# Four bf16 sums of the vector engine placed ahead of one fp32 add, in five slots of a fused attention and MLP kernel

## The chip, the cores and the metric

The kernel runs on one core of one Trainium2 chip. The metric is the device time of one execution in microseconds (us); the figure of a kernel is the median of its runs. The engines are called as in the profile: PE (matrix multiply), PEld (its weight loads), DVE (vector), ACT (scalar, activation functions), POOL (GpSimd) and SP (here only a DMA queue). L723 is line 723 of the kernel's file.

## What is computed

Inputs are `x` (8 batches, 8 heads, 512 tokens, 64 wide), `state` (8, 8, 32, 64), `w_in` (512 x 2048) and `w_out` (2048 x 512). Per batch and head:

```
a     = softmax(x @ state^T / 8);   xread = a  @ state      # 512 rows
a2    = softmax(state @ x^T / 8);   sread = a2 @ x          # 32 rows
rows  = concat(xread, sread), heads side by side            # 544 x 512 per batch
out   = gelu(rows @ w_in) @ w_out                           # exact gelu
```

The output is 4352 x 512 in fp32. Nearly all the work is the two products with `w_in` and `w_out`.

## The kernel before

**Staging.** The program is written out by hand in the order in which every engine is to run it: each engine takes its own instructions in program order, and semaphores join the engines. After a start phase (batches 0 and 1) the loop at L1224 runs over batches b = 2 to 7, and in each over eight slots p = 0 to 7. A slot holds two hidden tiles of batch b and one product that finishes batch b-1.

**Hidden tiles, `M(k)` (`mm1`, L501).** Two PE matmuls of 128x512 into a PSUM tile `hp`, then a Gelu on ACT into `gs[b][:, m, :]` (L513). Sixteen tiles m make a batch. The left operand is `P`, which is `state @ w_in` of the batch. `hp` shares a ring of four PSUM buffers (`ps_f`, tag `f`) with other tiles, half of the `P` products among them.

**Second matmul, `X(b, name)` (L672).** The 512 x 2048 by 2048 x 512 product of a batch is cut in a Strassen-Winograd scheme into seven products named "1" to "7", each of sixteen 128x256 matmuls (L647) into one of four PSUM banks (`otile` 0 to 3). Their left operands are quarters of `g` or sums of quarters (`g_sum`, L629). Products "1", "6", "5", "7" of batch b-1 run in slots 0 to 3 of batch b, product "3" in slot 5, and product "4" of batch b itself in slot 7. After product "7" DVE makes two adds (`c22`, `c21`, L702 and L705). After product "3" it makes one add, `oh <- xp, u` (L699, recorded at L666), which reads PSUM bank 2 and is followed by an output DMA on SP.

**Product "2"** of batch b is done by a second level of the same scheme (`sub_a`, L738, and `sub_b`, L745; matmuls of 128x128 at L729). It needs four sums of bf16 pieces of 128x512 elements, named 5, 6, 7, 3 in that order (`sub_sums`, L715; the DVE instruction is L723, tile `gsub`). They read only tiles m = 0 to 7 of batch b, which are done by slot 3. Sum 6 reads sum 5, sum 3 reads sum 6. `sub_a` uses sum 5, `sub_b` the other three.

**Slots 3 to 6 in batches 2 to 6, in program order:** slot 3: `M` tiles, product "7" with its two adds, then sum 5 (L1264). Slot 4: two tiles. Slot 5: two tiles with product "3" (in odd batches between the two tiles) and its add (L1296); then sums 6, 7, 3 (L1299); then `p_all` (L988), which makes `P` of the next batch: in even batches first the `reads_mm` products (L964), then four groups f of eight matmuls (L441) into PSUM tiles, where group 3's first tile is bank 2, then six copies to bf16 (L1004), three on ACT and three on DVE; then `rearr_ones` (L235), two bf16 copies on POOL, which wait in even batches for the `reads_mm` products that read their target and in odd ones for a `hold` on a Gelu; then `sub_a`; then two more ACT copies (L1310). Slot 6: two tiles, `sub_b`. The second hidden tile of slot 6 takes the PSUM buffer that the first DVE copy of `p_all` empties.

POOL also does `rearr` (L225), two bf16 copies, once an `x` batch has landed.

Of the kernel before, what the change touches and what calls it, by code (L numbers as in the profile page):

```python
# [10 lines left out]
BF16 = mybir.dt.bfloat16  # L11
# [6 lines left out]
def kernel(  # L18
# [8 lines left out]
    nc = tc.nc  # L27
# [17 lines left out]
    apool = ctx.enter_context(tc.tile_pool(name="apool", bufs=3))  # L45
# [230 lines left out]
    def xtr_dma(b):  # L276
        A = atts[b]
        nc.sync.dma_start_transpose(
            out=A.xT.rearrange("p j c n -> p (j c) n"),
            in_=A.x4.rearrange("p j c n -> p (j c n)"),  # L280
        )
# [43 lines left out]
    def scores(b, half):  # L325
        A = atts[b]
        if half == 0:
            begin_e(b)
        pt = ps_f.tile([128, SJ, 2, 2, NS], FP32, name="pt", tag="f")
        for ci in range(2):  # L330
            c = 2 * half + ci
            for j in range(SJ):
                nc.tensor.matmul(  # L333
                    pt[:, j, :, ci, :],
                    lhsT=A.xT[:, j, c, :],
                    rhs=sbd[:, b, c, :],
                    start=True,
                    stop=True,
                )
        nc.scalar.activation(  # L340
            out=A.e[:, :, 64 * half:64 * half + 64],
            in_=pt.rearrange("p j t c n -> p (j t) (c n)"),
            func=AF.Exp,
            scale=scale,
        )

    def norm(b, half):
        A = atts[b]
        G = SJ * 2
        hs = slice(64 * half, 64 * half + 64)  # L350
        e4 = A.e[:, :, hs].rearrange("p g (c n) -> p g c n", n=NS)
        cs = att.tile([128, G, 2], FP32, name="cs", tag="cs")
        nc.vector.reduce_sum(out=cs, in_=e4, axis=AX.X)  # L353
        ics = att.tile([128, G, 2], FP32, name="ics", tag="ics")
        nc.vector.reciprocal(out=ics, in_=cs)
        nc.vector.tensor_tensor(  # L356
            out=A.a[:, :, hs].rearrange("p g (c n) -> p g c n", n=NS),
            in0=e4,
            in1=ics[:, :, :].to_broadcast((128, G, 2, NS)),
            op=ALU.mult,  # L360
        )
# [16 lines left out]
    def atr_dma(b):  # L378
        A = atts[b]
        A.AT = att.tile([128, SJ, 2, 128], BF16, name="AT", tag="AT")  # L380
        nc.sync.dma_start_transpose(
            out=A.AT.rearrange("p j t n -> p (j t) n"), in_=A.a
        )
# [173 lines left out]
    MH = MC // 2  # L557
# [44 lines left out]
    xs = {}  # L602
# [12 lines left out]
    def chain(name, q, got):  # L615
        a11, a12, a21, a22 = q(0, 1), q(0, 0), q(1, 1), q(1, 0)
        return {
            "1": (a11,),
            "2": (a12,),
            "4": (a22,),  # L620
            "5": (a21, a22, ALU.add),
            "6": (got.get("5"), a11, ALU.subtract),
            "7": (a11, a21, ALU.subtract),
            "3": (a12, got.get("6"), ALU.subtract),
        }[name]
# [3 lines left out]
    def g_sum(b, names, home=None):  # L629
        got = g_lhs.setdefault(b, {})  # L630
        for name in names:
            x, y, op = chain(name, lambda h, k: g_q(b, h, k), got)
            if home is None:
                got[name] = apool.tile([128, MH, 256], BF16, name="gsum", tag="gsum")
            else:
                got[name] = home
            nc.vector.tensor_tensor(out=got[name], in0=x, in1=y, op=op)  # L637
# [70 lines left out]
    def sub_q(b):  # L708
        def q(h, k):
            g = g_q(b, 0, 0)  # L710
            return g[:, MH // 2 * k:MH // 2 * k + MH // 2, 128 * h:128 * h + 128]

        return q

    def sub_sums(b, names):  # L715
        if "5" in names:
            xs[b, "subs"] = apool.tile([128, 4, MH // 2, 128], BF16, name="gsub", tag="gsum")
            xs[b, "sub"] = {}
        got = xs[b, "sub"]
        for name in names:  # L720
            x, y, op = chain(name, sub_q(b), got)
            got[name] = xs[b, "subs"][:, "5673".index(name)]
            nc.vector.tensor_tensor(out=got[name], in0=x, in1=y, op=op)  # L723

    def sub_mm(b, name, at, start=False):
        lhs = chain(name, sub_q(b), {})[0] if name in "124" else xs[b, "sub"][name]
# [174 lines left out]
    def r_homes():  # L901
        pair = [att.tile([128, 2, MH, 128], BF16, name="rs", tag="xT") for _ in range(2)]
        homes = [pair[0][:, 0], pair[0][:, 1], pair[1][:, 0], pair[1][:, 1]]
        rs["homes"] = dict(zip("5673", homes))
        rs["lhs"] = {}

    def r_sum(names):
        got = rs["lhs"]
        for name in names:
            x, y, op = chain(name, r_q, got)  # L910
            got[name] = rs["homes"][name]
            nc.vector.tensor_tensor(out=got[name], in0=x, in1=y, op=op)
# [104 lines left out]
    def hold_for(b, m):  # L1017
        nc.gpsimd.tensor_copy(out=hold, in_=gs[b][:, m, 0:1])  # L1018


    def M(*ms):
        for m in ms:
            mm1(m // MC, m % MC)
# [200 lines left out]
    for b in range(2, B):  # L1224
        nb = b + 1
        for p in range(8):
            k = 16 * b + 2 * p
            if p == 1 and nb < B:
                scores(nb, 0)
                scores(nb, 1)  # L1230
            if p in (2, 3) and nb < B and (b > 2 or p == 2):
                norm(nb, p - 2)
            if p == 3 and nb + 1 < B:
                xtr_dma(nb + 1)
            if p == 5 and nb < B:
                atr_dma(nb)
            if nb == B and p < 5:
                read_out_slot(p)
                if p == 4:
                    r_homes()  # L1240
                    r_sum("56")
                continue
            late = p == 5 and b % 2 and nb < B
            if late:
                M(k)
            elif b != 2 or p != 3:
                M(k, k + 1)
            if b == 2 and p == 2:
                M(k + 2, k + 3)
            if b == 2 and p == 1:  # L1250
                w_diff("7")
            if p < 5 and nb < B:
                if p == 0:
                    g_sum(b - 1, "56")
                if p == 2:
                    if b % 2:
                        srts((b - 1, b))
                    g_sum(b - 1, "7")
                if p == 3:
                    g_sum(b - 1, "3")  # L1260
                if p < 4:
                    X(b - 1, "1657"[p])
                if p == 3:
                    sub_sums(b, "5")  # L1264
                if b == 2 and p == 2:
                    norm(3, 1)
                    for x in [(2, f, p_mm(2, f, ftile)) for f in (2, 3)]:
                        p_copy(*x)
                if p == 1 and b > 2:
                    sr_w("5216"[b - 3])  # L1270
            if p == 0 and b + 3 < B:
                hold_for(b, 0)
                load_x(4 if b == 2 else b + 3)
            if p == 6 and b == 2:
                hold_for(b, 12)
                load_x(5)
            if p == 0 and nb + 1 < B:
                begin(nb + 1)
                rearr(nb + 1)
            if nb == B:  # L1280
                if p == 5:
                    R("2")
                    r_sum("73")
                    R("4")
                    sub_sums(b, "5673")
                if p == 6:
                    R("1")
                    sub_a(b)
                    R("6")
                    sub_b(b)  # L1290
                    R("5")
                if p == 7:
                    X(b, "4")
                continue
            if p == 5:
                X(b - 1, "3")  # L1296
                if late:
                    M(k + 1)
                sub_sums(b, "673")  # L1299
                reads = (b, nb) if b % 2 == 0 else ()  # L1300
                rest = p_all(nb, reads)
                if b == 2:
                    rearr_ones(4)
                elif nb + 1 < B:
                    if not reads:
                        hold_for(b, 11)
                    rearr_ones(nb + 1)
                sub_a(b)
                for _, f, ps in rest:
                    nc.scalar.copy(out=Ps[nb][:, 0, f * 512:(f + 1) * 512], in_=ps[0])  # L1310
            if p == 6:
                sub_b(b)
            if p == 7:
                if nb == B - 1:
                    srts(reads)
                X(b, "4")
    b = B - 1
# [42 lines left out]
```

## Time and profile before

| | |
|---|---|
| median of 3 runs | 204.64 us (204.28, 204.64, 204.72) |
| profiled execution | 204.2 us, of which the span from first to last instruction is 202.3 us |
| granted PE clock | 1.000 throughout |
| PE busy | 193.9 us, 96% of the span |
| DVE busy | 157.3 us, 78% |
| ACT busy | 145.8 us, 72% |
| POOL busy | 49.9 us, 25% |
| sums L723 (24 of them) | 409 ns the shortest, about 417 ns the median, 1255 ns the longest |
| add after product "3" in batches 2 to 6 | 0.69 us each |

The share of busy time says which engine has most to do, not which one is late: PE's 96% holds matmuls that are pipelined and whose ends are modelled. What decides is, stretch by stretch, which engine waits for which. The views used are the table of waits (engine, line, releaser), the timeline (instructions in order of time, with the idle time before each and what ended it), and the busy time of the engines within chosen stretches. Times in them are microseconds from the start of the span.

### The profile page before, as it was taken

The page shows a single profiled execution, that of the slowest core. Times are in us where ns is not written, and L with a number is a line of the kernel's source. Part 1 is how long each engine was busy: PE and PEld are TensorE (multiplying, and loading weights), DVE is VectorE, ACT ScalarE, POOL GpSimd, SP SyncE. Part 2 cuts the span into 40 slices and gives each one's busy share as a digit, 9 for nine tenths or more (in the row PEclk, how much of TensorE's full clock was granted, in tenths as well). Part 3 has the DMA queues.
Part 4 walks back from the last instruction along what each step waited for, and adds up shares of the span by engine and source line. Part 5 has one row for each costly group of instructions (what it writes and reads, how often), then busy time and mean ns, then how long its engine had stood idle before and what let it go on. Part 6 is the DMA issues. An engine that isn't in the chain of part 4 may idle for free.

```text
span 202.3 us, 5055 instructions
## 1 busy us (share of the span) xinstructions
PE 193.9 (96%) x2102; PEld 134.1 (66%) x2107; DVE 157.3 (78%) x279; ACT 145.8 (72%) x264; POOL 49.9 (25%) x65
## 2 busy tenths in 40 slices
PE   7899999999999899999999799999999999999993
PEld 2434544466867587767767577667776787878893
DVE  2963896879987979966996978759948797984863
ACT  3875678798994989669966798499957777775220
POOL 8972403634322444041405300040000000000000
PEclk9999999999999999999999999999999999999999
DMA  6999999987486989680988016240125010040054
GB/s 202 182 177 201 209 196 202 195 152 135 54 140 149 165 102 148 120 209 0 102 160 209 3 34 126 106 104 0 55 76 135 0 54 1 3 156 0 11 151 156
DMA packets 40567, 23.16 MB, mean 115 GB/s; under 512 B 21856, under 2 KB 39136, under 8 KB 40544
## 3 DMA queue, kind: packets, MB, share of 16 engines
q0 software_dynamic: 13984, 8.10, 29.8%
q1 hardware_dynamic: 25728, 14.22, 28.2%
q10 hardware_dynamic: 832, 0.52, 0.8%
q8 instruction: 16, 0.26, 0.6%
q14 instruction: 7, 0.06, 0.1%
HBM read 17.30 MB, written 8.91 MB: 130 GB/s over the span
## 4 chain that ended last, share of the span: by engine, by line
PE 83%; DMA 5%; DVE 4%; POOL 4%; ACT 2%; issue 0%; POOLq 0%
PE xp L647 36%; PE hp L506 26%; DMA xb<-in_x_dram 5%; PE xp L729 4%; PE op L548 3%; PE sp L868 3%; PE rp L934 3%; DVE gsub L723 3%; POOL w_in_bf L105 2%; PE op L532 2%; PE xp L775 2%; PE pt L333 2%; PE p_ps L441 1%; POOL sbd L95 1%; DVE oh L666 1%; ACT P L1004 1%
## 5 line engine op out<-in xcount | busy, mean ns | idle before, releaser
L513 ACT ACTIVATE g<-hp 128x512 bf16<-128x512 f32 x124 | 67.1, 612 | 17.5 <-PE hp L506 17.3
L506 PE MATMUL hp<-AT,P 128*128 128x512 bf16 x248 | 62.5, 380 | 2.0 <-DVE P L1004 2.0
L647 PEld LDWEIGHTS <-gsum 128*128 128x128 bf16 x416 | 40.4, 98 | 8.9 <-issue 0.4
L647 PE MATMUL xp<-ws,gsum 128*128 128x256 bf16 x320 | 38.2, 273 | 0.0
L506 PEld LDWEIGHTS <-P 128*128 128x128 bf16 x248 | 22.9, 98 | 21.8 <-issue 3.2
L647 PEld LDWEIGHTS <-g 128*128 128x128 bf16 x240 | 23.3, 98 | 4.8
L637 DVE TENSOR_TENSOR gsum<-g 128x2048 bf16<-128x2048 bf16 x14 | 17.5, 1250 | 0.6 <-ACT g L513 0.6
L225 POOL COPY x<-xb 128x1024 bf16<-128x1024 bf16 x12 | 13.0, 1110 | 19.2 <-DMA xb<-in_x_dram 19.2
L235 POOL COPY xo<-xb 128x1024 bf16<-128x1024 bf16 x12 | 12.8, 1093 | 14.2 <-PE sr L964 14.0
L647 PE MATMUL xp<-w_out_bf,g 128*128 128x256 bf16 x128 | 15.3, 273 | 0.0
L1018 POOL COPY hold<-g 128x1 bf16<-128x1 bf16 x7 | 2.8, 405 | 43.2 <-ACT g L513 43.2
L647 PE MATMUL xp<-ws,g 128*128 128x256 bf16 x112 | 13.4, 273 | 0.0
L666 DVE TENSOR_TENSOR oh<-xp,c 128x512 f32<-128x512 f32 x14 | 9.6, 686 | 4.1 <-PE xp L647 3.9
L548 PE MATMUL op<-w_out_bf,g 128*128 128x512 bf16 x44 | 11.1, 380 | 0.5 <-issue 0.3
L666 DVE TENSOR_TENSOR oh<-xp,u 128x512 f32<-128x512 f32 (+2 forms) x9 | 5.2, 573 | 8.1 <-PE xp L647 7.8
L647 PE MATMUL xp<-w_out_bf,gsum 128*128 128x256 bf16 x96 | 11.5, 273 | 0.0
L356 DVE TENSOR_TENSOR a<-e,ics 128x512 bf16<-128x512 bf16 x14 | 10.2, 732 | 0.5
L353 DVE TENSOR_REDUCE cs<-e 128x16 f32<-128x512 bf16 x14 | 9.5, 679 | 0.9 <-ACT e L340 0.9
L1004 DVE CAST P<-p_ps 128x512 bf16<-128x512 f32 x15 | 9.4, 680 | 0.0
L666 DVE TENSOR_TENSOR c<-qb 128x256 f32<-128x256 f32 x6 | 2.6, 426 | 8.4 <-ACT qb L751 8.3
L513 ACT ACT_TABLE_LOAD x7 | 9.0, 1283 | 0.1
L441 PE MATMUL p_ps<-w_in_bf,sbd 64*32 64x512 bf16 x248 | 9.1, 381 | 0.0
(155 smaller groups left out, 314.6 us busy)
## 6 DMA issues: line engine op xcount, KB each, us to landing
out_dram<-oh SPq DMA_DIRECT2D x15, 256.0 KB, 3.2
xb<-in_x_dram POOLq DMA_DIRECT2D x7, 512.0 KB, 7.6
out_dram<-oh SPq DMA_DIRECT2D x6, 512.0 KB, 3.4
w_in_bf<-in_moe_w_in_dram POOLq DMA_DIRECT2D x6, 256.0 KB, 11.5
out_dram<-osb SPq DMA_DIRECT2D x5, 256.0 KB, 3.0
w_out_bf<-in_moe_w_out_dram POOLq DMA_DIRECT2D x4, 256.0 KB, 7.6
w_out_bf<-in_moe_w_out_dram POOLq DMA_DIRECT2D x2, 512.0 KB, 13.3
x0f<-in_x_dram SPq DMA_DIRECT2D x3, 256.0 KB, 3.7
```

What stands on the lines that cost most here:

```text
L225: nc.gpsimd.tensor_copy(out=A.x4[:, :, :, 64 * t:64 * t + 64].rearrange("p j c d -> p c j d"), in_=src[:, t],)
L235: eng.tensor_copy(out=A.xo[:, :, :, 2 + 64 * t:66 + 64 * t].rearrange("p j c d -> p c j d"), in_=src[:, t],)
L353: nc.vector.reduce_sum(out=cs, in_=e4, axis=AX.X)
L356: nc.vector.tensor_tensor(out=A.a[:, :, hs].rearrange("p g (c n) -> p g c n", n=NS), in0=e4, in1=ics[:, :, :].to_broadcast((128, G, 2, NS) ...
L441: nc.tensor.matmul(ps[t][32 * c:32 * c + 32, :], lhsT=sbd[64 * t:64 * t + 64, b, c, 32 * t:32 * t + 32], rhs=w_in_bf[64 * t:64 * t + 64, c ...
L506: nc.tensor.matmul(hp, lhsT=Ps[b][:, t, m * 128:(m + 1) * 128], rhs=atts[b].AT[:, :, t, :], start=(t == 0), stop=(t == 1),)
L513: nc.scalar.activation(out=gs[b][:, m, :], in_=hp, func=AF.Gelu)
L548: nc.tensor.matmul(ops[b, j], lhsT=gs[b][:, m, j * 128:(j + 1) * 128], rhs=w_out_bf[:, m, :], start=(m == 0), stop=(m == MC - 1),)
L637: nc.vector.tensor_tensor(out=got[name], in0=x, in1=y, op=op)
L647: nc.tensor.matmul(ps[:, j - js[0], :], lhsT=lhs[:, m, 128 * j:128 * j + 128], rhs=rhs[:, m, :], start=(first and j == js[0] and m == 0), ...
L666: nc.vector.tensor_tensor(out=out, in0=x, in1=y, op=ALU.add)
L1004: copy(out=Ps[b][:, t, f * 512:(f + 1) * 512], in_=ps[t])
```

## The change

The sums 6, 7 and 3 move up to sum 5, into slot 3. In program order of DVE they then stand before the add that follows product "3" and no longer behind it. This happens in batches 2 to 6. In batch 7 all four were already together. The tile, its buffers and the operands stay the same, and the order of the instructions of PE, ACT, POOL and SP is the same in both programs; on DVE the add goes from second to fifth place in each of the five groups.

```diff
-    def sub_sums(b, names):
-        if "5" in names:
-            xs[b, "subs"] = apool.tile([128, 4, MH // 2, 128], BF16, name="gsub", tag="gsum")
-            xs[b, "sub"] = {}
-        got = xs[b, "sub"]
-        for name in names:
+    def sub_sums(b):
+        t = apool.tile([128, 4, MH // 2, 128], BF16, name="gsub", tag="gsum")
+        got = xs[b, "sub"] = {}
+        for i, name in enumerate("5673"):
             x, y, op = chain(name, sub_q(b), got)
-            got[name] = xs[b, "subs"][:, "5673".index(name)]
-            nc.vector.tensor_tensor(out=got[name], in0=x, in1=y, op=op)
+            got[name] = t[:, i]
+            nc.vector.tensor_tensor(out=t[:, i], in0=x, in1=y, op=op)
...
                 if p == 3:
-                    sub_sums(b, "5")
+                    sub_sums(b)
...
-                    sub_sums(b, "5673")
+                    sub_sums(b)
...
                 X(b - 1, "3")
                 if late:
                     M(k + 1)
-                sub_sums(b, "673")
                 reads = (b, nb) if b % 2 == 0 else ()
```

## The prediction

> **What bounds the kernel now.** I read the table of waits first, for PE alone and from 50 to 200 us, since the changed loop lies there. It has one row for a PE matmul:
>
> ```profile
> PE hp L506 <- DVE P L1004: 2.0, 2, 1.4
> ```
>
> Two waits, 2.0 us together, the longer 1.4, both for a DVE copy of `P` out of PSUM. Elsewhere in that stretch PE's matmuls follow one another. The chain of waits agrees: from 50 to 200 us it is PE nearly throughout, except where it passes through add, three sums and first copy on DVE (65.2 to 69.0 and 108.2 to 112.8 us), and through ACT for about 1 us each in batches 3, 5 and 6.
>
> Second, the busy times in one same stretch of each of the five slots: from the first matmul of `sub_a` to the first of `sub_b`. PE does the same there each time: 16 matmuls of `sub_a`, then two hidden tiles, 4 matmuls.
>
> ```profile
> 66.92:69.48 2.56, 1.92 (x20) 1.28 (x20) 2.56 (x4) 2.40 (x6) 0.87 (x1) 1.00 1.25 135
> 88.58:90.33 1.75, 1.75 (x20) 1.28 (x20) 1.75 (x4) 1.59 (x4) 1.75 (x2) 1.00 0.92 225
> 109.92:113.23 3.31, 1.91 (x20) 1.28 (x20) 3.31 (x4) 2.99 (x6) 3.12 (x3) 1.00 0.42 116
> 132.33:134.08 1.75, 1.75 (x20) 1.28 (x20) 1.75 (x4) 1.59 (x4) 1.75 (x2) 1.00 0.67 197
> 153.56:155.31 1.75, 1.75 (x20) 1.28 (x20) 1.75 (x4) 1.59 (x4) 0.00 (x0) 1.00 0.44 142
> ```
>
> Rows are batches 2 to 6; after the bounds stand the length, then PE, PEld, DVE, ACT and POOL busy. The same twenty matmuls take 1.75 us in three slots and 2.56 and 3.31 in batches 2 and 4. I use these lengths and not the waits' 0.64 and 1.40, because a matmul's modelled end runs past the start of the next: in batch 2 the hidden tile could have started at 67.82 + 0.43 = 68.25 and started at 69.05, which is 0.80.
>
> Third, the timeline of batch 4, for what makes the copy late:
>
> ```profile
> 106.20 0.42 DVE L723 TENSOR_TENSOR gsub<-g 128x512 bf16<-128x512 bf16 x1
> ...
> 108.19 0.69 DVE L666 TENSOR_TENSOR oh<-xp,u 128x512 f32<-128x512 f32 x1 [1.58 <-PE xp L647]
> 108.48 2.22 POOL L235 COPY xo<-xb 128x1024 bf16<-128x1024 bf16 x2 [10.04 <-PE sr L964]
> ...
> 108.80 0.99 DVE L723 TENSOR_TENSOR gsub<-gsub,g 128x512 bf16<-128x512 bf16 x1
> ...
> 109.72 1.25 DVE L723 TENSOR_TENSOR gsub<-g 128x512 bf16<-128x512 bf16 x1
> ...
> 110.65 2.40 POOL L225 COPY x<-xb 128x1024 bf16<-128x1024 bf16 x2
> ...
> 110.90 1.25 DVE L723 TENSOR_TENSOR gsub<-g,gsub 128x512 bf16<-128x512 bf16 x1
> ...
> 112.07 1.87 DVE L1004 CAST P<-p_ps 128x512 bf16<-128x512 f32 x3
> 112.80 0.59 PE L506 MATMUL hp<-AT,P 128*128 128x512 bf16 x2 [1.40 <-DVE P L1004]
> ```
>
> DVE sat idle for 1.58 us before the add, then ran three sums, of 0.42 us when alone, in 0.99, 1.25 and 1.25 us beside POOL's copies; only then came the first copy that the hidden tile waits for. In batch 2 it is 1.07, 1.25 and 0.41. In batches 3, 5 and 6 the three are 0.41 to 0.42 us each, done before or without POOL's copies. The cast, beside POOL's copies in batch 3, keeps 1.88 us for three, and the add its 0.69: operations that read PSUM are not stretched, sums with both operands in SBUF are. On this, the Trainium skill ("SBUF — State Buffer", Who interferes with whom) says that a vector instruction with two SBUF inputs contends with a GpSimd instruction that reads SBUF and that the loser blocks for the whole instruction; 1.25 against 0.42 us agrees, and by it a sum that begins behind a POOL copy pays that copy's rest whatever its own size, so moving the sums only helps where the new place has no POOL copy.
>
> **The change, part by part.** Nothing is added or removed. On DVE, the three sums go from behind the add to in front of it, in five slots; PE, ACT, POOL and SP keep their order, so no DMA moves in any queue.
>
> *Do the sums fit into the idle time?* In batch 7 all four stand back to back already, starting at 181.53, 181.98, 182.33, 182.66, and the next instruction at 183.00: 1.47 us from the start of sum 5. Sum 5 starts at 63.75, 85.47, 106.20, 128.99 and 149.73; plus 1.47 the add could start at 65.22, 86.94, 107.67, 130.46 and 151.20. It starts now, when product "3" ends, at 65.21, 87.02, 108.19, 130.77 and 151.94. So the add is late by 0.01 us in batch 2 and by nothing in the others; spare are 0.08, 0.52, 0.31 and 0.74. The data are there: the moved sums read the same hidden tiles as sum 5.
>
> The Trainium skill speaks against the fit ("VectorE: DVE Perf Modes", The DRAIN you can't avoid): the next operation does not start until the pipe of the one before it is empty. Laid end to end, four sums of 0.42 would be 1.68 and the add 0.2 us late in batch 2; the rows overlap by about 0.08 us, and in batch 2 those 0.2 would still hide in front of the copy, so that the sum would be the same by both.
>
> *Is POOL quiet there?* Its timeline has nothing between 61.6 and 65.56, between 80.5 and 88.18, from 98.4 to 108.48, from 113.1 to 131.93, or from 134.4 on. In batches 2 and 4 POOL's copies cannot begin before `reads_mm`, which PE runs only after product "3", the very thing the add waits for. So all moved sums cost 0.42.
>
> *Who queues behind the add?* Before: three sums, then copies. After: the copies at once. They need `P` products: L441 runs 65.76 to 66.82 in batch 2 in four groups, and the first DVE copy takes one of the second group, so about 66.35; it ends near 67.0, where the tile wants its buffer at 68.25. In batch 4 the same gives 109.35 to 110.0 against 111.24. Both waits go.
>
> *What is late next?* ACT's copy `qa` in front of `sub_b`: it ends at 68.60 in batch 2 and `sub_b` would start at 66.92 + 1.75 = 68.67; batches 3, 5 and 6 run with just this distance and no wait. So the stretch shrinks to 1.75: gains of 0.81 and 1.56 us.
>
> *Does the gain reach the end?* In batch 2 ACT has no pause from 68.0 to 72.04, so it moves forward only with its next copy, which idles 0.92 us before 72.96: more than 0.81. In batch 4 its pauses are 0.35 and 1.03, together 1.38 for 1.56; the difference is made up by the Gelu, which there runs in two parts. Batch 6, the same even slot without the stall, needs 5.35 us from `sub_a` to that copy with 0.23 idle (two small transposes of PE, 0.11 us, among it), so ACT follows. The sums of `g` for product "6" (DVE, ending at 74.7) are needed at 76.86 - 0.81. The DMA transposes that feed the next batch land, by their issue times and the longest landings (5.3 us for `AT`, 7.0 for `xT`), 2 us or more before their first use, also when that comes earlier by the gain. After batch 4 all engines move together.
>
> *Batches 3, 5, 6:* PE waits there for ACT or nothing; DVE's earlier copies are hidden: 0.
>
> *Sum:* 0.81 + 1.56 = 2.37 us. The profiled execution had 204.20 us (span 202.3 and 1.9 around it), so 201.83; it lies 0.44 below the median of the runs, and on the median of 204.64 the sum gives 202.27. I take the latter.
>
> **The rivals.**
>
> *Part of it is given back in batch 3.* POOL's `rearr` copies there start at 78.05, when an `x` batch lands; that load was issued behind a Gelu of batch 2 that does not move, while DVE's work around it comes 0.81 us earlier. DVE has no pause from 75.57 to 85.89, and the sum for product "7" (79.96, 1.65 us instead of 1.22) ends at 81.61. If it cannot end earlier, product "7" starts near 81.70 and not at 82.03 - 0.81 = 81.22: 0.48 back, 202.75. If everything of batch 2 is lost, 203.1. Against it: the multiply at 78.38 was itself held 0.56 us by the same copies and now starts before them.
>
> *The sums do not matter:* the tile waits for something that ends with the copy by chance. 204.6. Against it, in both slots PE starts 0.04 us after the first copy's end.
>
> *Slower: the sums become what holds PSUM bank 2.* The add now stands behind them, and the first tile of `P` group 3 waits for it. If POOL copies run over the moved sums, each takes 1.25: 3 x 0.83 = 2.49 more. In batch 3, less 0.08 spare and less 0.34 (the group's other tile waits anyway for a Gelu ending 88.05, the add ends 87.71), PE loses 2.07; in batch 5, by its spare 0.31, 1.84. One slot leaves 204.3; with both, 206.2. It decides from two slots on. Against it, POOL ends 5.4 us before the sums of batch 3 and 16 us before those of batch 5.
>
> **How the numbers follow.** Full gain 0.76, around 202.3 (201.8 to 202.6 by the spread of the runs before and the low profiled one); part given back 0.14 (202.6 to 203.1); no effect 0.04 (204.6); slower 0.05 (206.2); more than the sum 0.01. The range 201.7 to 203.1 leaves about 0.1 out, and takes in both bounds of what batch 3 may give back. About 0.2% (0.4 us) is what a measurement of this kernel tells from no change: faster 0.91, same 0.04, slower 0.05.
>
> **What would show it.** Right: in the profile after, all 24 sums take about 0.42 us; add starts unchanged against product "3"; the row of PE waiting for the DVE copy is gone; the five stretches are all 1.75 us. The first step fails if an add starts more than 0.1 us after product "3" ends; the last fails if the stretches are 1.75 and PE waits anew in batch 3 for the sum of product "7", or for ACT after batch 4.

## The result, and the profile after

| | before | changed |
|---|---|---|
| median (lowest to highest) of 6 runs each | 204.37 us (203.99 to 204.72) | 202.26 us (201.81 to 202.63) |
| profiled execution | 204.20 us, span 202.3 | 202.25 us, span 200.3 |
| DVE busy | 157.3 us | 155.1 us |
| POOL busy | 49.9 us | 48.1 us |

The changed kernel takes 0.9898 of the time of before (95% interval 0.9880 to 0.9915): faster by 2.1 us. PE's busy time is 193.9 us in both; what went is idle time.

The table of waits for PE from 50 to 198 us is empty. The five stretches from the first matmul of `sub_a` to that of `sub_b`, in the same columns as before (length, then PE, PEld, DVE, ACT and POOL busy; rows are batches 2 to 6):

```profile
67.39:69.14 1.75, 1.75 (x21) 1.28 (x20) 1.72 (x5) 1.59 (x4) 0.57 (x1) 1.00 1.22 117
88.23:89.98 1.75, 1.75 (x20) 1.28 (x20) 1.38 (x3) 1.59 (x4) 1.75 (x2) 1.00 0.88 230
109.52:111.27 1.75, 1.75 (x21) 1.28 (x20) 1.72 (x5) 1.59 (x4) 1.75 (x3) 1.00 0.45 150
130.37:132.12 1.75, 1.75 (x21) 1.28 (x20) 1.37 (x3) 1.59 (x4) 1.75 (x2) 1.00 0.67 196
151.60:153.35 1.75, 1.75 (x20) 1.28 (x20) 1.72 (x5) 1.59 (x4) 0.00 (x0) 1.00 0.44 144
```

All are 1.75 us now; batches 2 and 4 had 2.56 and 3.31. The timeline of batch 4 in the changed kernel (start, length, engine, line; in brackets the idle time before and what ended it):

```profile
105.85 0.41 DVE L721 TENSOR_TENSOR gsub<-g 128x512 bf16<-128x512 bf16 x1
...
106.30 0.42 DVE L721 TENSOR_TENSOR gsub<-gsub,g 128x512 bf16<-128x512 bf16 x1
...
106.64 0.42 DVE L721 TENSOR_TENSOR gsub<-g 128x512 bf16<-128x512 bf16 x1
106.98 0.42 DVE L721 TENSOR_TENSOR gsub<-g,gsub 128x512 bf16<-128x512 bf16 x1
...
107.85 0.69 DVE L666 TENSOR_TENSOR oh<-xp,u 128x512 f32<-128x512 f32 x1 [0.45 <-PE xp L647]
108.14 2.03 POOL L235 COPY xo<-xb 128x1024 bf16<-128x1024 bf16 x2 [10.04 <-PE sr L962]
...
109.13 1.88 DVE L1002 CAST P<-p_ps 128x512 bf16<-128x512 f32 x3 [0.59 <-PE p_ps L441]
```

The four sums take 0.42 us each and are over before POOL starts; the add still waits 0.45 us for product "3"; and the copy of `P`, which began at 112.07, now waits for its own matmuls and begins at 109.13. POOL's two copies take 2.03 us and not 2.22, since no sum delays them.

Where the 2.4 us inside the loop lie shows best in the distances between the starts of `sub_a` in successive batches; the last column runs to the first matmul of PE's last group (product "3" of batch 7). Programs that are alike up to that point start `sub_a` of batch 2 at different times: 66.92 us before and 67.43 in the kernel with the sums moved in batches 3, 5 and 6 only; 67.39, 67.55, 67.13 and 67.49 in the changed kernel, its repetition and two more that differ from it only later. The start phase alone thus differs by up to 0.5 us from one execution to the next, a good part of the spread of the runs (0.73 and 0.82 us in the table). Distances leave that out.

| us from `sub_a` of one batch to the next | 2 to 3 | 3 to 4 | 4 to 5 | 5 to 6 | 6 to 7 | `sub_a` of 2 to the last group |
|---|---|---|---|---|---|---|
| before | 21.66 | 21.34 | 22.41 | 21.23 | 28.98 | 130.40 |
| changed | 20.84 | 21.29 | 20.85 | 21.23 | 28.98 | 127.96 |
| the changed kernel a second time, below | 20.85 | 21.31 | 20.85 | 21.24 | 28.98 | 128.00 |

0.82 after batch 2, 0.05 after batch 3, 1.56 after batch 4, nothing later: 2.44. The 0.05 is not clear of the scatter; the same distance is 21.35 and 21.36 in two kernels below that have no stall either.

### The profile page after: what moved, and what is told of

Same layout as the page of the kernel before. It is cut to its first block, busy times and chain, and to the rows that moved or that the text cites. A ratio compares the mean times of both kernels' runs of the same rounds, so it can differ in the third digit from the quotient of the medians.

```text
span 200.3 us, 5055 instructions
## 1 busy us (share of the span) xinstructions
PE 193.9 (97%) x2102; PEld 134.3 (67%) x2107; DVE 155.1 (77%) x279; ACT 145.6 (73%) x264; POOL 48.1 (24%) x65
## 4 chain that ended last, share of the span: by engine, by line
PE 86%; DMA 5%; POOL 4%; ACT 2%; issue 0%; DVE 0%; POOLq 0%
PE xp L647 36%; PE hp L506 26%; DMA xb<-in_x_dram 5%; PE xp L727 5%; PE op L548 3%; PE sp L866 3%; PE rp L932 3%; POOL w_in_bf L105 2%; PE op L532 2%; PE xp L773 2%; PE pt L333 2%; ACT P L1002 1%; PE p_ps L441 1%; PE sr L962 1%; POOL sbd L95 1%; POOL w_out_bf L113 1%
## 5 line engine op out<-in xcount | busy, mean ns | idle before, releaser
L637 DVE TENSOR_TENSOR gsum<-g 128x2048 bf16<-128x2048 bf16 x14 | 17.0, 1218 | 0.6 <-ACT g L513 0.6
L225 POOL COPY x<-xb 128x1024 bf16<-128x1024 bf16 x12 | 12.2, 1044 | 18.5 <-DMA xb<-in_x_dram 18.5
L235 POOL COPY xo<-xb 128x1024 bf16<-128x1024 bf16 x12 | 12.2, 1043 | 14.1 <-PE sr L962 13.9
L1016 POOL COPY hold<-g 128x1 bf16<-128x1 bf16 x7 | 2.3, 334 | 42.9 <-ACT g L513 42.9
L637 DVE TENSOR_TENSOR gsum<-gsum,g 128x2048 bf16<-128x2048 bf16 x7 | 8.6, 1225 | 0.2
```

Source lines behind the costliest of these rows:

```text
L225: nc.gpsimd.tensor_copy(out=A.x4[:, :, :, 64 * t:64 * t + 64].rearrange("p j c d -> p c j d"), in_=src[:, t],)
L235: eng.tensor_copy(out=A.xo[:, :, :, 2 + 64 * t:66 + 64 * t].rearrange("p j c d -> p c j d"), in_=src[:, t],)
```

## The experiments

**The theory:** the price of before is two waits of PE, in batches 2 and 4, for a copy of `P`. The copy is late because three sums stand in front of it, each held up by POOL's copies. **The rivals:** every slot gives its share; the place behind the add costs by itself, POOL or not; and, for the limits of the change, the question what a late add would cost.

### Only in the slots that stalled, and only in the others

```diff
                 if p == 3:
-                    sub_sums(b, "5")
+                    sub_sums(b, "5673" if b in (2, 4) else "5")
...
-                sub_sums(b, "673")
+                if not (b in (2, 4)):
+                    sub_sums(b, "673")
```

> The three sums move only in batches 2 and 4; batches 3, 5 and 6 keep the order of before. Theory (the gain is the two waits of PE, 0.81 and 1.56 us, and nothing else): as the changed kernel, 2.1 to 2.4 us below before, near 202.2. Rival (every slot gives its share, two fifths of the measured 2.1): 0.85 below before, near 203.5.

Measured: 202.06 us, 0.9888 of before (0.9874 to 0.9903), and PE has no wait in the loop. The mirror has `b in (3, 5, 6)` in both places:

> The mirror: the sums move only in batches 3, 5 and 6. Theory: no change from before within 0.2 us, near 204.4, and the two waits of PE for the copy of P stay at 0.6 and 1.4 us. Rival (every slot gives its share): 1.3 below before, near 203.1.

Measured: 204.24 us, 1.0002 of before (0.9989 to 1.0016). Its table of waits for PE keeps the row of before:

```profile
PE hp L506 <- DVE P L1004: 2.1, 2, 1.4
```

The distances agree: 21.65, 21.34, 22.42, 21.24 where the sums move in 3, 5 and 6, and 20.86, 21.36, 20.85, 21.23 where they move in 2 and 4. So the whole gain comes from two of the five slots, and the rival of equal shares falls.

### The order of before, without the collision

```diff
                 rest = p_all(nb, reads)
+                if b in (2, 4):
+                    nc.gpsimd.tensor_copy(out=hold, in_=Ps[nb][:, 0, 512:513])
```

> The order of before, sums behind the add, but in batches 2 and 4 the POOL copies (xo) are held by a one-column POOL copy of P until ACT's third copy of P is done, about 67.9 and 110.4 us, so that the sums run before them. Theory (the price comes from the sums' collision with POOL, 0.42 stretched to 1.25 us, not from their place as such): in batch 2 the first copy then ends near 67.6 where the tile wants it at 68.25, in batch 4 near 110.5 against 111.24, no wait, 2.0 to 2.4 below before, near 202.3. Rival (the place behind the add costs by itself, POOL or not): at most 0.5 below before, 203.9 to 204.4.

Measured: 201.87 us, 0.9883 of before (0.9870 to 0.9896). The sums still stand behind the add. Batch 4 of this kernel:

```profile
107.38 0.69 DVE L666 TENSOR_TENSOR oh<-xp,u 128x512 f32<-128x512 f32 x1 [1.58 <-PE xp L647]
...
107.99 0.42 DVE L723 TENSOR_TENSOR gsub<-gsub,g 128x512 bf16<-128x512 bf16 x1
...
108.32 0.42 DVE L723 TENSOR_TENSOR gsub<-g 128x512 bf16<-128x512 bf16 x1
...
108.66 0.42 DVE L723 TENSOR_TENSOR gsub<-g,gsub 128x512 bf16<-128x512 bf16 x1
...
108.99 1.88 DVE L1004 CAST P<-p_ps 128x512 bf16<-128x512 f32 x3
...
110.22 2.09 POOL L235 COPY xo<-xb 128x1024 bf16<-128x1024 bf16 x2
```

DVE's idle 1.58 us before the add is unused here as it was before, three sums follow the add, and yet the copy comes in time. The place behind the add was harmless; what cost was POOL's copies beginning 0.3 us after the add. Moving the sums is one way to part them, holding POOL is another.

### Both cures, and the changed kernel again

```diff
+                if b in (2, 4):
+                    nc.gpsimd.tensor_copy(out=hold, in_=Ps[nb][:, 0, 512:513])
```

added to the changed kernel behind `p_all`, and beside it the changed kernel itself:

> Both cures at once: the sums moved in every slot, and POOL's copies in batches 2 and 4 held until ACT's third copy of P. Theory (both remove the same two waits, and PE has no other from 50 to 198 us): as the changed kernel within 0.3 us, near 202.2. Rival (the hold gives something of its own, since the run with the hold alone was the fastest so far): 0.3 to 0.5 below the changed kernel, near 201.8.

> The changed kernel itself, beside the others on the same chip, so that the three near 202 can be compared: 202.0 to 202.5.

Measured: 201.92 us, 0.9864 of before (0.9827 to 0.9901), with both; 202.51 us, 0.9890 (0.9850 to 0.9930), the changed kernel. The intervals lie over one another, and PE waits in neither. From `sub_a` of batch 2 to the last group the one with both takes 128.18 us and the changed kernel 128.00; the hold alone 128.19. Inside the loop the hold thus costs about 0.2 us more and the lower medians go with an earlier start (`sub_a` of batch 2 at 66.91 and 67.01 against 67.39 and 67.55 us). That the hold itself makes the start earlier is not to be seen, since it is not yet in effect there. By the medians alone, 0.59 us apart, the rival would have it; by the distances inside the loop the theory holds. No version is shown to beat the changed kernel.

### How much room is left before the add

One sum more behind the four, then three more, first in all five slots and then only where POOL is quiet. The results of the added sums go nowhere. The diff is that of three in all five; the others have `if b in (3, 5, 6)` or one added sum, with operands of the same size.

```diff
             nc.vector.tensor_tensor(out=t[:, i], in0=x, in1=y, op=op)
+        if b < B - 1:
+            for i in (0, 2, 3):
+                nc.vector.tensor_tensor(
+                    out=extra.rearrange("p (m n) -> p m n", m=4), in0=t[:, 0], in1=t[:, i], op=ALU.add
+                )
```

> The changed kernel with three more sums of 0.42 us (pitch 0.34 to 0.45, about 1.05 together) behind the four, in batches 2 to 6 (their result is used by nothing). It measures how much room the idle time before the add still has. Theory, from the profile of the changed kernel: spare before the add 0, 0.24, 0.45, 0.23 and 0.67 us in batches 2 to 6, so the add is late by 1.05, 0.81, 0.60, 0.82 and 0.38; the first tile of group 3 of P waits for the add in batch 2 (about 0.5 us) and, less the 0.34 us in which the group waits for a Gelu anyway, in batches 3 and 5 (about 0.45 each), not in 4 and 6: 1.2 to 1.6 above the changed kernel, near 203.7. Rival A (a late add costs nothing while the copy of P is in time): 202.3. Rival B (every late microsecond of the add is paid in full): 3.7 above, near 206.

Measured: 206.06 us over twelve runs, 1.0063 of before (1.0028 to 1.0097). The seven runs with a granted clock of 0.999 or 1.000 have a median of 205.84 us, 3.3 to 3.6 above the two medians of the changed kernel; the other five, at 0.983 to 0.992, took 207.29 to 209.93. The expectation failed, and the time came where rival B had it. But not for its reason. The start of the added sums and the wait of PE in batch 2:

```profile
65.19 2.89 DVE L725 TENSOR_TENSOR extra<-gsub 128x512 bf16<-128x512 bf16 x3
65.59 2.22 POOL L236 COPY xo<-xb 128x1024 bf16<-128x1024 bf16 x2 [4.04 <-PE sr L968]
...
68.00 0.68 DVE L667 TENSOR_TENSOR oh<-xp,u 128x512 f32<-128x512 f32 x1
...
68.74 0.41 PE L442 MATMUL p_ps<-w_in_bf,sbd 64*32 64x512 bf16 x8 [2.11 <-DVE oh L667]
```

I had priced the added sums at 0.42 us. In batches 2 and 4 they outlast product "3", meet POOL's copies and take 2.89 and 2.14 us together, against 1.34 in the other slots; PE waits, with the last group of `P`, for the add to free bank 2. From the start of product "3" to `sub_a` batch 2 takes 5.80 us against 3.76 (2.04 lost), and the distances that lead into batches 3, 4, 5 and 6 are longer by 0.48, 0.94, 0.48 and 0.02; I had expected 0.5 in batch 2, then 0.45, 0, 0.45 and 0. So a late add is not paid in full (rival B), and not free (rival A): where POOL is quiet the expected terms hold to 0.03.

> The three added sums only in batches 3, 5 and 6, where POOL is quiet. Theory, from the stretch between the end of product 3 and the start of the second level in the run with three more in every slot (2.21 us against 1.57 of the changed kernel in batch 3): 0.64 lost in batch 3, the same in batch 5, nothing in batch 6, so 1.3 above the changed kernel, near 203.6. Rival (all the added DVE time beyond the spare time before the add is paid, 1.25 less 0.24, 0.23 and 0.67): 2.6 above, near 204.9.

Measured: 203.07 us, 0.9921 of before (0.9895 to 0.9948). Its table of waits has one row for PE in the loop:

```profile
PE p_ps L442 <- DVE oh L667: 1.0, 2, 0.5
```

The distances are 0.47 longer into batch 3, 0.46 into 5, 0.03 into 6: 0.96, not the expected 1.3, and not the rival's 2.6. The 1.3 came from stretches that I had measured from a modelled matmul end in one kernel and from the next start in the other; from start to start the earlier run gives 0.48, too.

> The changed kernel with one more sum (0.42 us, its result used by nothing) behind the four in batches 2 to 6. The run with three more cost far more than expected because in batches 2 and 4 the added sums outlasted product 3 and met POOL's copies. One more ends at the start of those copies. Theory (the add may be late by up to the 0.5 us that the copy of P or the Gelu holds the group anyway): within 0.3 us of the changed kernel, near 202.3. Rival (any lateness of the add is paid): 0.35 in batch 2 and 0.1 in batches 3 and 5, 0.5 to 0.6 above, and more if POOL stretches the added sum.

Measured: 202.06 us, 0.9869 of before (0.9833 to 0.9905); the distances are those of the changed kernel (20.85, 21.35, 20.85, 21.24). One added sum is free.

### POOL copies over the moved sums

```diff
                 if p == 3:
+                    if b in (3, 5):
+                        nc.gpsimd.tensor_copy(out=hold, in_=xs[b - 1, "o", 1][:, 0, 0:1])
+                        for _ in range(4):
+                            nc.gpsimd.tensor_copy(
+                                out=dummy.rearrange("p (m n) -> p m n", m=2), in_=gs[b][:, 0:2, :]
+                            )
                     sub_sums(b)
```

> The changed kernel with four more POOL copies of 128x1024 bf16 in batches 3 and 5, started when the second add after product 7 is done, so that they run over the moved sums (the added copies' output is used by nothing). Theory, the rival of the prediction that would be slower: each of the last three sums takes about 1.25 us, the add is late by some 2.2 us, the first tile of group 3 of P waits for bank 2, and PE loses about 1.9 us in each of the two slots: 3.8 above the changed kernel, near 206.0. Rival (the add is off the path, since only the copy of P is waited for, which still comes in time): within 0.5 of the changed kernel, 202.3 to 202.8.

Measured: 204.82 us, 1.0034 of before (1.0017 to 1.0051). Batch 5, with the added copies on POOL:

```profile
127.74 0.42 DVE L722 TENSOR_TENSOR gsub<-g 128x512 bf16<-128x512 bf16 x1
128.19 1.27 DVE L722 TENSOR_TENSOR gsub<-gsub,g 128x512 bf16<-128x512 bf16 x1
129.39 1.25 DVE L722 TENSOR_TENSOR gsub<-g 128x512 bf16<-128x512 bf16 x1
130.56 1.25 DVE L722 TENSOR_TENSOR gsub<-g,gsub 128x512 bf16<-128x512 bf16 x1
131.74 0.68 DVE L667 TENSOR_TENSOR oh<-xp,u 128x512 f32<-128x512 f32 x1
```

The first added POOL copy begins at 128.15; each sum behind it takes three times its 0.42. The distance into batch 5 grows by 1.73 us (22.58 against 20.85). In batch 3 one of the three sums began 0.16 us before POOL's first copy and escaped (0.43, 1.26, 1.25 us), and the distance into it grows by 0.90. Together 2.6 instead of 3.8 us: the theory's mechanism, two thirds of its sum. With only two such slots the moved order is slower than before, so the limit of the change is real: it lives on POOL being quiet in the new place.

### The sums moved the other way

```diff
-                sub_sums(b, "673")
...
                 rest = p_all(nb, reads)
+                sub_sums(b, "673")
```

> The order of before, with the sums 6, 7 and 3 moved the other way, behind the copies of P. Theory: the hidden tile no longer waits for the copy, but the second half of the second level (which needs the three sums) waits instead, by about 1.3, 1.2, 2.2, 1.2 and 0.9 us in batches 2 to 6 against 0.81 and 1.56 in batches 2 and 4 of before: about 4.4 above before, near 208.8. Rival (only the place of the copy matters): as the changed kernel, near 202.3.

Measured: 210.32 us (208.47 to 210.93), 1.0262 of before (1.0215 to 1.0310). Two waits of PE in batch 4 of the profile:

```profile
115.87 0.40 PE L729 MATMUL xp<-q_w,gsub 128*128 128x128 bf16 x4 [1.58 <-DVE gsub L723]
116.54 0.57 PE L729 MATMUL xp<-w_out_bf,gsub 128*128 128x128 bf16 x4 [0.27 <-DVE gsub L723]
```

The copy of `P` is in time here as well, and PE waits for the sums in its place (nine waits, 4.2 us together; a tenth, of 0.8 us in batch 6, is put down to a copy on ACT). Against the changed kernel the five distances are longer by 1.37, 1.09, 3.87, 0.79 and 1.22 us where 1.3, 1.2, 2.2, 1.2 and 0.9 were expected; four of them are within 0.41. The remaining one, after batch 4, holds a dip of PE's granted clock that is told of at the end. The dip seems to account for the miss of the median, too: the only one of the six runs with a granted clock of 1.000 took 208.47 us, against 208.8 expected, and the five with 0.991 or 0.992 took 210.03 to 210.93. So the place of the copy alone does not decide: both the copy and `sub_b` must get what they need. Behind the copies the sums come too late for `sub_b`; in the idle time before the add they serve both.

## Why the prediction was right, point by point

*The time.* 202.3 forecast, 202.26 measured. The agreement to 0.04 us is in part luck: I put 2.37 us on a median of 204.64 us of three runs, and six runs have 204.37, of which 2.11 is the measured difference. In the profiled executions, from `sub_a` of batch 2 to the last group, the sum of 2.37 stands against 2.44; the profiled execution after started `sub_a` 0.47 us later, which hid some of it (204.20 to 202.25 is 1.95).

*The two terms.* 0.81 for batch 2 measured 0.82; 1.56 for batch 4 measured 1.56; the three other slots were 0, and the two half changes confirm it. The reading from start to start, and not the 0.64 and 1.40 of the waits, was needed for this.

*The fit into the idle time.* Right in batches 3 to 6. In batch 2 the add should have been late by 0.01 us, and the prediction's own sign of failure for this step, an add more than 0.1 us behind the end of product "3", came true. The lines:

```profile
64.25 0.41 DVE L721 TENSOR_TENSOR gsub<-g 128x512 bf16<-128x512 bf16 x1
...
65.71 0.68 DVE L666 TENSOR_TENSOR oh<-xp,u 128x512 f32<-128x512 f32 x1
...
66.94 1.89 DVE L1002 CAST P<-p_ps 128x512 bf16<-128x512 f32 x3 [0.56 <-PE p_ps L441]
```

From sum 5 to the add is 1.46 us, as taken from batch 7. But sum 5 began later, because the sum ahead of the two adds took 1.83 us beside a POOL copy (1.70 before), and product "3" ends at 65.54: the add is 0.17 late. It cost nothing, since DVE then idles 0.56 us for the matmuls of `P`; in the run with one more sum the add starts 0.42 us behind product "3" and DVE still idles 0.22 us.

*The data, POOL, and the queue behind the add.* All 24 sums take 0.41 to 0.43 us after. The copy starts 0.12 us after the estimate in batch 2 when the later start is taken off (66.94 - 0.47 = 66.47 against 66.35), and 0.18 in batch 4 (109.13, where `sub_a` begins 0.40 earlier than before, against 109.35). The Trainium skill's rule weighed there ("SBUF — State Buffer", Who interferes with whom: a vector instruction with two SBUF inputs contends with a GpSimd instruction that reads SBUF, for ports that only one of them can hold) agrees with every run. Over all twelve profiles 20 sums began while a POOL copy of 128x1024 was in progress; they took 0.73 to 1.27 us, and each ended 0.27 to 0.28 us after that copy's end. All other sums took 0.41 to 0.43, also those that began shortly before a copy and ran on beside it. So the prediction's "done before or without POOL's copies" was not quite the point for batches 3 and 5: there the last sum (88.30 and 132.05) overlaps with a copy that began at 88.58 and 132.12, and keeps its 0.42. What counts is which of the two begins first. The other rule ("VectorE: DVE Perf Modes", The DRAIN you can't avoid), read as four sums end to end of 1.68 us, did not show: they need 1.46. The same section adds that a next operation that is not held starts earlier, which the prediction left out.

*What is late next.* `qa` and ACT did not hold `sub_b` in any slot, nor PE later.

*The first rival (batch 3 gives part back).* It did not come. POOL's `rearr` copies began at 76.93 there, 1.1 us earlier than before, and held the multiply (78.04, 1.51 us), not the sum:

```profile
78.04 1.51 DVE L356 TENSOR_TENSOR a<-e,ics 128x512 bf16<-128x512 bf16 x1
79.47 0.41 DVE L429 COPY XSR<-srT 128x256 bf16<-128x256 bf16 x1
79.80 1.21 DVE L637 TENSOR_TENSOR gsum<-g 128x2048 bf16<-128x2048 bf16 x1
```

The sum for product "7" ended at 81.01, and the product began at 81.69: the 81.22 of a full gain, plus the 0.47 by which this execution started `sub_a` of batch 2 later. My reason against the rival, that the multiply would start ahead of the copies, was wrong: the batch of `x` landed earlier than in the profile before. That load took 7.33 us from issue to landing there and 5.64 to 5.85 in the eleven other profiles, among them the one with the sums moved in 3, 5 and 6 only, which has the order of before in batch 2. So the late landing was a chance of one profile and not the kernel's habit, and the rival, whose condition was a late landing, was not put to the test. In the profile after, the collision fell on an instruction with room behind it.

*The slower rival.* Its mechanism was forced and is real, its price was near: 1.84 us said for batch 5, 1.73 measured with all three sums held. For batch 3 the 2.07 was not reached, since one sum slipped through; the same working with two sums held gives 2 x 0.83 - 0.08 - 0.34 = 1.24, and 0.90 was measured. Of the 0.34 too much, 0.16 is the spare time, which was 0.24 us in the profile after and not 0.08.

## What to carry to other kernels

Before moving an instruction off a late chain, look at what stretches it: here the same three sums cost nothing in three slots and 0.8 and 1.6 us in two, and keeping POOL's copies away from them brought as much as moving them. Read the loss from start to start of the waiting engine's instructions over a stretch that repeats, and compare it with a slot that has no stall; that gave both terms to 0.01 us. The idle time in front of a waiting instruction is a good home for work as long as that instruction is not made later than those behind it can bear: one sum more was free, though it made the add 0.42 us late in batch 2; three more cost 0.5 us in two of the three slots where nothing else ran and nothing in the third, and 2.0 and 0.9 us where they ran into the other engine's copies.

## What had not been expected of the hardware

A DVE sum that meets a row of POOL copies seems to wait for the copy in progress and then to go ahead of the next: in the run with added copies the sums start 1.2 us apart, each ends about 0.27 us after a copy's end, and the four POOL copies take 4.57 us, 1.14 each, against 1.02 when alone. That the two take turns is read from these lengths and was not tried by itself. The cost is uneven: a sum grows by 0.84 us, a copy by 0.12.

In the run with the sums behind the copies, PE was busy for only 0.29 and 0.13 us in the two microseconds from 114 to 116, and its granted clock then was 0.81 from 116 to 117, 0.50 to 120, 0.98 to 121 and 1.00 again (the figure behind POOL's count is the clock):

```profile
114.00:115.00 1.00, 0.29 (x2) 0.00 (x0) 1.00 (x2) 1.00 (x4) 0.93 (x1) 1.00 0.06 15
115.00:116.00 1.00, 0.13 (x3) 0.14 (x4) 0.96 (x5) 1.00 (x3) 0.00 (x0) 1.00 0.00 0
116.00:117.00 1.00, 0.73 (x9) 0.56 (x8) 0.48 (x2) 0.02 (x1) 0.00 (x0) 0.81 0.00 0
117.00:118.00 1.00, 1.00 (x7) 0.63 (x6) 0.00 (x0) 0.43 (x1) 0.00 (x0) 0.50 0.00 0
```

Some 3.5 us at half speed is about 1.7 us, which is the 3.87 less the expected 2.2 in that batch. Waits of 1.40 us before, and of 2.11 in the run with three more sums, left the clock of their profiles at 1.00. It is not a matter of the program alone: the mean granted clock was 0.991 or 0.992 in five of the six runs of this kernel and 1.000 in the sixth, 0.983 to 0.992 in five of the twelve with three more sums, 0.992 in two of seventeen of before beside them, and never under 0.999 in the twelve runs of the changed kernel. That the wait of PE brings the dip about, and what decides whether it comes, is not shown; but in the profile in which it came the batch lost more than the wait that had been expected.
